# Sliding-window attention with an MLP on one core: weight loads on SP's queue, row-sum adds on ACT, sink copies first, and a new list for the first 21 steps

## The chip, the cores and the metric

The kernel runs on one core of one Trainium2 chip. The metric is the device time of one execution in microseconds (us). The kernel before was timed three times: 725.0, 724.87 and 722.57, median 724.87. A further execution, the one that was profiled, took 722.06.

## The reference

```python
def _attn_ref(q, k, v, n_sink, window):          # q, k, v: 4 x 8 x 768 x 64
    scores = scale * np.matmul(q, k.transpose(0, 1, 3, 2))
    keep = is_sink | in_window                   # first 4 keys, or the last 128 positions
    scores = np.where(keep, scores, -1000000000.0)
    scores = scores - np.max(scores, axis=-1, keepdims=True)
    a = np.exp(scores)
    a = a / (np.sum(a, axis=-1, keepdims=True) + 1e-09)
    return np.matmul(a, v)

def _moe_ref(x, w_in, w_out):                    # x: 3072 x 512, w_in: 512 x 2048
    h = x @ w_in
    g = np.maximum(h, 0.0) + np.log1p(np.exp(-np.abs(h)))
    return g @ w_out                             # w_out: 2048 x 512
```

The attention's output, heads side by side, is the `x` of the second part: softplus between two matrix products. The inputs are float32 except that the weights reach the kernel as 64-bit words.

## The kernel before, in words

**Tiling.** The 3072 tokens are 12 chunks of 256 rows, three for each of the four batches. A chunk has eight heads of attention (a head and chunk together are a *step*, 96 in all), and then, in slices that lie between the attention steps of the following chunk, the MLP: eight slices of 256 of the 2048 hidden columns. All weights stay in SBUF: 32 half blocks, `wi00` to `wi71` of w_in and `wo00` to `wo71` of w_out (the first digit is the slice, the second the half), each loaded as 512 KB of 64-bit words and turned into a high and a low part (`fp32r`), so that a product is three matmuls, high by high, low by high, high by low. Chunks 0 and 1 do their scores and values on plain float32 operands; from chunk 2 on these are split in two parts as well.

**What one step issues.** Each part has a letter that the list below uses, followed by a number (the step, or for `U F P R D E` the chunk's slice).

- `S` scores (L255 in chunks 0 and 1, L258 and L259 later): PE matmuls into `s`.
- `T` softmax: DVE masks the block above the diagonal (L271) and takes a masked row maximum (L277), ACT the exponential with its row sum `sm` (L278); each for two blocks of 128 rows.
- `N` normalise: 1e-9 is added to `sm` (L284, DVE), the reciprocal `rc` is taken (L285, DVE), the weights are multiplied by it (L290 on ACT, L292 on DVE or POOL).
- `W` weights_t: PE turns the weights (L326), a copy `th` of them is made (L59 on ACT, L61 on DVE), POOL makes the two triangles `pt` of it (L337, L340).
- `k` and `K`: the four sink keys' weights of four heads (`sa`, L297, DVE), turned by PE (`ts`, L308) and copied by ACT into the two halves of `sk` (L59). From chunk 2 on DVE subtracts each half from its source right behind its copy (L67). In chunks 0 and 1 POOL clears `sk` first (L311).
- `V` values: PE (L356, L362); `O` out: ACT writes the high part `xh` and DVE the low part `xl` of two heads of the MLP's input (L59, L67).
- `U` up: 24 matmuls `h` of a slice (L488); `F` softplus: three ACT passes (L495 to L497); `P` gate: maximum and sum on DVE (`mt`, L503) and its high part `gh`; `R`: the low part `gl` (DVE, L67); `D` and `E`: the slice's matmuls into `acc` (L525 to L527).
- `w`, `a`, `c`, `d`, `l`: the next half block of weights: its load (`_weight_dma`, L387 to L400), the cast of its words' top (`upper`), the combination with the rest (L432, DVE), the cast to the high part and the subtraction that gives the low part (L67).
- `G`, `L`, `j`, `J`, `p`, `q`: loads of values, keys and queries, of the sinks, and the splits of chunk 2's inputs.

**What sets the order.** `START` is a string of 362 such tokens that is written out by hand for the first 21 steps; behind it a loop over `STEADY` places the parts of each later step in a fixed order. On PE and SP (`ORDERED`) instructions stand exactly in the order of the tokens; on DVE, ACT and POOL a scheduler sets them at build time. All five engines then run their queues in order. Tables name the engine of the n-th operation of a kind (A is ACT, V is DVE, P is POOL; the last letter holds for all that follow): `NM` the multiply, `TH` the copy `th`, `GH` the cast `gh`, `WT` the cast of the top, `WH` the high part, `WL` the low part.

**Queues.** Keys, queries, values and results are issued by SP (`nc.sync.dma_start`, L200, L202, L207, L227), weights by ACT (`nc.scalar.dma_start`, L397), in ACT's own order of instructions, at 0.34 us for each issue. A transfer has one of eight completion semaphores in turn (`DMAHW0` to `DMAHW7` in the order of instructions below), and a new one waits until the transfer that last used its semaphore has landed.

Of the kernel before, what the change touches and what calls it, by code (L numbers as in the profile page):

```python
# [133 lines left out]
class _Attention:  # L134
# [145 lines left out]
    def normalise(self, h):  # L280
# [3 lines left out]
        nc.vector.tensor_scalar(sm[:], sm[:], 1e-9, None, ALU.add)  # L284
# [590 lines left out]
Ctx.START = """
S0 G4 T0 w w S1 j4 T1 J0 w L8 w w S3 S2 N0 N1 T2 W0 L10 w N2 S4 T3 N3 a w T4 k0 a c K0 a S5 c W1 w w
d S6 V0 O0 l d V1 w c l T5 N4 W2 T6 d w a S7 c O1 W3 l N5 G6 N6 a T7 c V2 N7 a d S8 k4 a O2 W4 w T8
c V3 S9 O3 w w K4 d l l V4 W5 N8 L12 w O4 c T9 S10 W6 d T10 N9 V5 l O5 a c G8 S11 W7 d l T11 L14 w
W8 G10 V6 N10 V7 O6 N11 a c O7 d l w k8 a U0 w c a S12 d a l d w T12 c w d l l K8 V8 c F0 N12 O8 P0
a c d R0 l d a c w W9 U1 a S13 c F1 T13 l a d c l d a P1 l N13 d c D0 l w R1 a c G12 w V9 w w d L16  # L880
O9 l W10 U2 a w d S14 F2 a c l T14 c d l P2 d l N14 W11 a L17 c V10 a w c E0 U3 p16 O10 d w w w l w
R2 F3 d D1 a S15 E1 a T15 w c a P3 c E2 d a d c d G14 l N15 V11 c l l L18 O11 k12 l d U4 l W12 a S16
p17 F4 K12 R3 T16 c a D2 a a l D3 V12 d c c N16 P4 L19 O12 p18 S17 W13 c R4 a U5 d F5 l a E3 d T17 c
V13 l N17 c G16 P5 W14 p19 L20 l J16 O13 U6 D4 S18 F6 E4 d l T18 L21 R5 P6 l W15 R6 p20 U7 d D5 F7 d
# [55 lines left out]
```

## Time and profile before

| | |
|---|---|
| three runs | 725.0, 724.87, 722.57 us (median 724.87) |
| the profiled execution | 722.06 us |
| its span, from the first to the last instruction | 720.4 us |
| busy: PE, DVE, ACT, POOL | 692.9 (96%), 549.0 (76%), 453.1 (63%), 399.8 (56%) us |
| mean clock granted to PE | 0.992 |
| first matmul of slice 0 of chunk 0 (`U0`) | 40.05 us |
| first matmul of slice 0 of chunk 1 (`U8`, the last but a few in `START`) | 110.97 us |

PE is the engine for matmuls and PEld its weight loads, which overlap the matmuls; DVE, ACT and POOL are the vector, scalar and general engines; ACTq and SPq are the places where ACT and SP issue DMAs. `128x512 fp32r<-128x512 f32 x5 | 5.9, 1186 | 0.5 <-ACT wo L59 0.5` reads: five instructions of that shape, 5.9 us busy, 1186 ns each in the mean, 0.5 us of idle time of the engine ahead of them, and what ended most of it. Line numbers are those of the kernel before.

### The profile page before, as it was taken

The page shows a single profiled execution, that of the slowest core. Times are in us where ns is not written, and L with a number is a line of the kernel's source. Part 1 is how long each engine was busy: PE and PEld are TensorE (multiplying, and loading weights), DVE is VectorE, ACT ScalarE, POOL GpSimd, SP SyncE. Part 2 cuts the span into 40 slices and gives each one's busy share as a digit, 9 for nine tenths or more (in the row PEclk, how much of TensorE's full clock was granted, in tenths as well). Part 3 has the DMA queues.
Part 4 walks back from the last instruction along what each step waited for, and adds up shares of the span by engine and source line. Part 5 has one row for each costly group of instructions (what it writes and reads, how often), then busy time and mean ns, then how long its engine had stood idle before and what let it go on. Part 6 is the DMA issues. An engine that isn't in the chain of part 4 may idle for free.

```text
span 720.4 us, 13834 instructions
## 1 busy us (share of the span) xinstructions
PE 692.9 (96%) x4465; PEld 618.6 (86%) x4465; DVE 549.0 (76%) x1596; ACT 453.1 (63%) x1122; POOL 399.8 (56%) x769
## 2 busy tenths in 40 slices
PE   4788899999999999999999999999999999999996
...
GB/s 299 333 244 262 168 45 47 130 48 46 102 66 50 108 68 49 113 59 51 100 52 67 79 78 56 95 65 57 94 53 71 97 50 79 60 13 1 30 1 34
DMA packets 41204, 63.36 MB, mean 88 GB/s; under 512 B 4644, under 2 KB 22692, under 8 KB 41124
## 3 DMA queue, kind: packets, MB, share of 16 engines
...
## 4 chain that ended last, share of the span: by engine, by line
PE 90%; DVE 3%; ACT 2%; DMA 2%; POOL 1%; issue 1%; SPq 0%; ACTq 0%; POOLq 0%
PE h L488 37%; PE acc L525 12%; PE acc L527 12%; PE acc L526 12%; PE x L362 6%; PE t L326 3%; PE s L258 3%; PE s L259 3%; PE x L356 2%; DMA wo71r<-w 1%; DMA q<-q 1%; ACT a L278 1%; DVE sm L284 1%; DMA words<-sizes 1%; DVE wt L432 0%
## 5 line engine op out<-in xcount | busy, mean ns | idle before, releaser
L488 PE MATMUL h<-xh,wi 128*128 128x256 f32 x1536 | 254.0, 288 | 0.0
L488 PEld LDWEIGHTS h<-xh,wi 128*128 128x128 f32 x1536 | 211.6, 191 | 1.2 <-issue 0.3
L488 PE MATMUL h<-xl,wi 128*128 128x256 f32 x768 | 154.6, 283 | 0.0
L525 PE MATMUL acc<-wo,gh 128*128 128x512 f32 x384 | 153.2, 399 | 0.0
L527 PE MATMUL acc<-wo,gl 128*128 128x512 f32 x384 | 151.2, 394 | 0.9 <-DVE gl L67 0.9
L526 PE MATMUL acc<-wo,gh 128*128 128x512 f32 x384 | 151.2, 394 | 0.0
L63 POOL TENSOR_SCALAR gh<-mt 128x512 fp32r<-128x512 f32 x91 | 57.3, 629 | 165.7 <-DVE mt L503 136.8
L495 ACT ACTIVATE mt<-h 128x512 f32<-128x512 f32 x96 | 57.5, 599 | 106.2 <-PE h L488 104.5
L292 POOL TENSOR_SCALAR a<-a,rc 128x128 f32<-128x128 f32 x180 | 72.4, 415 | 85.6 <-DVE rc L285 54.3
L488 PEld LDWEIGHTS h<-xl,wi 128*128 128x128 f32 x768 | 119.6, 192 | 0.0
L503 DVE SCALAR_TENSOR_TENSOR mt<-h,mt 128x512 f32<-128x512 f32 x96 | 65.8, 686 | 47.4 <-ACT mt L497 35.5
L278 ACT ACTIVATE a<-a,stats 128x136 f32<-128x136 f32 x192 | 76.0, 396 | 34.5 <-DVE stats L277 34.4
L527 PEld LDWEIGHTS acc<-wo,gl 128*128 128x128 f32 x384 | 72.4, 189 | 17.9 <-DVE gl L67 1.3
L525 PEld LDWEIGHTS acc<-wo,gh 128*128 128x128 f32 x384 | 72.4, 188 | 13.0 <-issue 0.5
L526 PEld LDWEIGHTS acc<-wo,gh 128*128 128x128 f32 x384 | 72.6, 189 | 9.3
L67 DVE TENSOR_TENSOR gl<-mt,gh 128x512 fp32r<-128x512 f32 x96 | 76.6, 798 | 4.9 <-POOL gh L63 4.6
L496 ACT ACTIVATE mt<-mt 128x512 f32<-128x512 f32 x96 | 60.8, 633 | 3.1
L497 ACT ACTIVATE mt<-mt 128x512 f32<-128x512 f32 x96 | 60.7, 633 | 3.1
L59 ACT CAST qkh<-qk 128x656 fp32r<-128x656 f32 x80 | 59.3, 741 | 1.5 <-DMA qk<-qk 1.4
L67 DVE TENSOR_TENSOR kl<-qk,qkh 128x400 fp32r<-128x400 f32 x80 | 52.3, 654 | 2.5
L271 DVE COPY_PREDICATED s<-diag,s 128x128 f32<-128x128 int32 x160 | 41.8, 290 | 15.4 <-PE s L259 12.5
L337 POOL TENSOR_SCALAR_AFFINE_SELECT pt<-th 128x256 fp32r<-128x256 f32 (+1 forms) x96 | 46.6, 486 | 8.0 <-DVE th L61 5.0
...
## 6 DMA issues: line engine op xcount, KB each, us to landing
...
out<-o SPq DMA_DIRECT2D x24, 256.0 KB, 2.6
q<-q SPq DMA_DIRECT2D x8, 256.0 KB, 5.9
...
k<-k SPq DMA_DIRECT2D x8, 200.0 KB, 4.4
wi00r<-w ACTq DMA_DIRECT2D x1, 511.8 KB, 4.8
wi01r<-w ACTq DMA_DIRECT2D x1, 511.8 KB
```

The source lines that it names most:

```text
L59: nc.scalar.copy(out, in_)
L67: (nc.vector if eng == "V" else nc.gpsimd).tensor_tensor(out, a, b, ALU.subtract)
L278: nc.scalar.activation(a, a, AF.Exp, bias=nm, scale=-1.0, accum_out=sm[:, j : j + 1])
L292: (nc.vector if eng == "V" else nc.gpsimd).tensor_scalar(a, a, rc[:, j : j + 1], 0.0, ALU.mult, ALU.add)
L488: nc.tensor.matmul(h[:, j], wt, x, start=k == 0, stop=k >= len(prods) - 2, skip_group_check=True)
L495: nc.scalar.activation(t[:], h[:], AF.Abs)
L496: nc.scalar.activation(t[:], t[:], AF.Exp, scale=-1.0)
L497: nc.scalar.activation(t[:], t[:], AF.Ln, bias=1.0)
L503: nc.vector.scalar_tensor_tensor(t[:], h[:], 0.0, t[:], ALU.max, ALU.add)
L525: nc.tensor.matmul(acc[:], gh[:, j, q], wh, start=f == 0, stop=False, skip_group_check=True)
L526: nc.tensor.matmul(acc[:], gh[:, j, q], wl, start=False, stop=False, skip_group_check=True)
L527: nc.tensor.matmul(acc[:], gl[:, j, q], wh, start=False, stop=f == 2 * FP - 1, skip_group_check=True)
```

## The change

Four edits are made together. The 1e-9 is added to the row sums by ACT (an Identity with a constant `tiny` as bias, which POOL writes once) where DVE did it, in all 96 steps. Both copies of `sk` are written ahead of the two subtractions. The 32 weight loads go to SP's queue, in the place of their `w` token among SP's other loads. `START` is a new order of the same 362 tokens, and the tables that name engines are new. `STEADY` is the same.

```diff
@@ normalise
-        nc.vector.tensor_scalar(sm[:], sm[:], 1e-9, None, ALU.add)
+        nc.scalar.activation(sm[:], sm[:], AF.Identity, bias=c.tiny[:, :1])
         nc.vector.reciprocal(rc, sm[:])
@@ sink
-        for j in range(CH):
-            r, q = slice(j * G * NS, (j + 1) * G * NS), slice(j * P, j * P + P)
+        places = [(slice(j * G * NS, (j + 1) * G * NS), slice(j * P, j * P + P)) for j in range(CH)]
+        for r, q in places:
             _copy(nc, "A", sk[r, q], t[r, :P])
-            if not self.exact:
+        if not self.exact:
+            for r, q in places:
                 _sub(nc, "V", sk[P // 2 + r.start : P // 2 + r.stop, q], t[r, :P], sk[r, q])
@@ _weight_dma
-        c.nc.scalar.dma_start(r[:, : 4 * WH - 1], src.bitcast(I16)[:, 1:])
+        c.nc.sync.dma_start(r[:, : 4 * WH - 1], src.bitcast(I16)[:, 1:])
@@ _kernel
+        c.tiny = c.const.tile([P, 1], F32, name="tiny")
+        nc.gpsimd.memset(c.tiny[:], 1e-9)
@@ tables
-Ctx.NM = "PPPAAPAPPVPPPPVVP"
-Ctx.TH = "AVAVAAAAVAAAAAVAVA"
-Ctx.GH = "VVVVVPPPP"
+Ctx.NM = "PPAPPPAAAAPPPPPPAPPPAP"
+Ctx.TH = "AAAAVVVAAVAAAAAAVAA"
+Ctx.GH = "PPVAAPAPAP"
-Ctx.WT = "PAAVVVVAVAAVAAAVAAAAAAAAAAAPAAAV"
-Ctx.WH = "VAPAAVAAAAVPPAAAAVVAVAAAAAVAVAAA"
-Ctx.WL = "PPPPPPPVPPVPPVPPVPVPPPPVVPVVPVPV"
+Ctx.WT = "VVAAPVPVAAPPAAPAAAAAAAAAAAAAAVAV"
+Ctx.WH = "AAPAAPAPPPAAVAVAAAAPAPAVPAAPAPAA"
+Ctx.WL = "VVPPVPPVVPPPPPVVPVVPVPVVVPPVVVVP"
@@ START, first line of ten
-S0 G4 T0 w w S1 j4 T1 J0 w L8 w w S3 S2 N0 N1 T2 W0 L10 w N2 S4 T3 N3 a w T4 k0 a c K0 a S5 c W1 w w
+S0 J0 w T0 N0 w w w w w L8 G6 S1 G4 T1 w j4 w S2 w L10 w w w T2 N1 L12 w w N2 L14 w W0 w w S3 T3 S4 T4 w a c a
```

Counted over `START` and by the tables, operations of each kind on each engine, before and after: multiplies by the reciprocal in 21 steps, two each: POOL 11 steps, ACT 3, DVE 3 before the table's last letter, and POOL 15, ACT 7; copies `th`: ACT 13, DVE 5, and ACT 14, DVE 5; casts `gh`: DVE 5, POOL 4, and POOL 5, ACT 4, DVE 1; tops: ACT 22, DVE 8, POOL 2, and ACT 21, DVE 6, POOL 5; high parts: ACT 21, DVE 8, POOL 3, and ACT 19, POOL 10, DVE 3; low parts: POOL 21, DVE 11, and DVE 17, POOL 15.

The first place is SP's queue where chunk 1's keys and queries (`k1_0` to `k1_6`, `q1_0` to `q1_6`) are loaded; `DMAHW` in brackets is the completion semaphore that the load waits for, `PE` that it waits for matmuls which read the buffer's former content. Before:

```order
L200 DMA k1_0_212<-k0 128x400 [waits DMAHW7_49]
L202 DMA q1_0_214<-q0 128x512 [waits DMAHW1_49]
L200 DMA k1_2_250<-k0 128x400 [waits DMAHW2_49,PE_49]
L202 DMA q1_2_252<-q0 128x512 [waits DMAHW3_49]
L227 DMA vr0_3_388<-v 128x2x128 [waits DMAHW4_49]
L200 DMA k1_4_481<-k0 128x400 [waits DMAHW7_49,DMAHW0_49,PE_49]
L202 DMA q1_4_483<-q0 128x512 [waits DMAHW1_49]
```

After, from `k1_4` on:

```order
L200 DMA k1_4_260<-k0 128x400 [waits DMAHW6_49,PE_49]
L202 DMA q1_4_262<-q0 128x512 [waits DMAHW7_49]
L398 DMA wo20r_264<-w 128x2047 [waits DMAHW0_49]
L398 DMA wo21r_266<-w 128x2047 [waits DMAHW1_49]
L200 DMA k1_6_272<-k0 128x400 [waits DMAHW2_49,PE_49]
L202 DMA q1_6_274<-q0 128x512 [waits DMAHW3_49]
L398 DMA wi40r_276<-w 128x2047 [waits DMAHW4_49]
L398 DMA wi41r_286<-w 128x2047 [waits DMAHW5_49]
L398 DMA wo30r_288<-w 128x2047 [waits DMAHW6_49]
```

Weight loads now stand between loads that wait for PE; of the 32, the twelve up to `wo21` are ahead of `k1_6` and the twenty from `wi40` on behind it.

The second place is ACT's queue around the sink weights of heads 0 to 3 (`sk0_0`), in the middle of chunk 0. Before, with weight loads among the casts:

```order
L397 DMA wi20r_275<-w 128x2047
L278 ACTIVATE a0_1_277,sm0_4_279<-a0_1_277,stats_63 128x136 x2
L59 CAST upper1_171<-wi01r_192 128x512
L59 COPY sk0_0_292<-ts0_0_290 32x128 x2
L59 CAST upper0_170<-wi10r_210 128x512
L397 DMA wi21r_311<-w 128x2047
L397 DMA wo10r_313<-w 128x2047
L59 CAST wi01_328<-wt0_0_1_301 128x512
L397 DMA wo11r_333<-w 128x2047
```

After, for the same place:

```order
L278 ACTIVATE a0_1_304,sm0_5_346<-a0_1_304,stats_63 128x136 x2
L59 CAST upper0_172<-wi10r_201 128x512
L59 CAST upper1_173<-wi11r_203 128x512
L59 COPY sk0_0_371<-ts0_0_369 32x128 x2
L284 ACTIVATE sm0_4_306<-sm0_4_306,tiny_66 128x2
L59 CAST wi01_380<-wt0_0_1_352 128x512
```

The loads have left the queue, and the add of head 4 stands behind the exponentials of head 5, two casts and the two copies of `sk`.

The third place is DVE's queue where slice 0 of chunk 0 is gated (`mt0_0`). Before:

```order
L432 SCALAR_TENSOR_TENSOR word_ps0_174<-wi30r_364,upper0_170 128x512
L61 CAST wi30_650<-word_ps0_174 128x512
L67 TENSOR_TENSOR wi30_650<-word_ps0_174,wi30_650 128x512
L432 SCALAR_TENSOR_TENSOR word_ps1_175<-wi31r_429,upper1_171 128x512
L284 TENSOR_SCALAR sm1_4_640<-sm1_4_640 128x2
L285 RECIPROCAL rc1_1_639<-sm1_4_640 128x2
L503 SCALAR_TENSOR_TENSOR mt0_0_666<-h0_0_596,mt0_0_666 128x512
L61 CAST gh0_0_677<-mt0_0_666 128x512
L432 SCALAR_TENSOR_TENSOR wt2_1_0_680<-wo20r_451,upper0_170 128x512
L67 TENSOR_TENSOR gl0_0_684<-mt0_0_666,gh0_0_677 128x512
```

After:

```order
L67 TENSOR_TENSOR wi30_638<-word_ps0_176,wi30_638 128x512
L433 SCALAR_TENSOR_TENSOR wt2_1_1_703<-wo21r_266,upper1_173 128x512
L504 SCALAR_TENSOR_TENSOR mt0_0_680<-h0_0_655,mt0_0_680 128x512
L61 CAST wo20_741<-wt2_1_0_684 128x512
L67 TENSOR_TENSOR wi31_653<-word_ps1_177,wi31_653 128x512
L433 SCALAR_TENSOR_TENSOR wt4_0_0_744<-wi40r_276,upper0_172 128x512
```

The cast `gh0_0`, the cast of `wi30` and the add of `sm1_4` have left DVE's queue; the reciprocal of head 4 of chunk 1 stands later in it. (`wt`, `word_ps0` and `word_ps1` are the combined words, `wi30r` is a half block as loaded, and the numbers behind the last underscore only tell tiles apart.)

More of the change, by code (lines that the diff above doesn't have):

```diff
@@ L396, in _weight_dma @@
     if c.w64:
-        c.nc.scalar.dma_start(r[:, : 4 * WH - 1], src.bitcast(I16)[:, 1:])
+        c.nc.sync.dma_start(r[:, : 4 * WH - 1], src.bitcast(I16)[:, 1:])
     else:
-        c.nc.scalar.dma_start(r[:, :WH], src)
+        c.nc.sync.dma_start(r[:, :WH], src)
     c.raw[s, k, half] = r
@@ L866 @@
 Ctx.GB, Ctx.EXACT = 3, 2
-Ctx.NM = "PPPAAPAPPVPPPPVVP"
-Ctx.TH = "AVAVAAAAVAAAAAVAVA"
-Ctx.GH = "VVVVVPPPP"
+Ctx.NM = "PPAPPPAAAAPPPPPPAPPPAP"
+Ctx.TH = "AAAAVVVAAVAAAAAAVAA"
+Ctx.GH = "PPVAAPAPAP"
 Ctx.WM = "sssssssppsppssssssssssssssssssss"
-Ctx.WT = "PAAVVVVAVAAVAAAVAAAAAAAAAAAPAAAV"
-Ctx.WH = "VAPAAVAAAAVPPAAAAVVAVAAAAAVAVAAA"
-Ctx.WL = "PPPPPPPVPPVPPVPPVPVPPPPVVPVVPVPV"
-Ctx.STEADY = ("kWUqYpKSFTRDVPONE", "SWTkpUKERDNFPqYVO")
-Ctx.START = """
-S0 G4 T0 w w S1 j4 T1 J0 w L8 w w S3 S2 N0 N1 T2 W0 L10 w N2 S4 T3 N3 a w T4 k0 a c K0 a S5 c W1 w w
@@ L877 @@
[L877 to L881, printed above, removed]
@@ L882 @@
-R2 F3 d D1 a S15 E1 a T15 w c a P3 c E2 d a d c d G14 l N15 V11 c l l L18 O11 k12 l d U4 l W12 a S16
-p17 F4 K12 R3 T16 c a D2 a a l D3 V12 d c c N16 P4 L19 O12 p18 S17 W13 c R4 a U5 d F5 l a E3 d T17 c
-V13 l N17 c G16 P5 W14 p19 L20 l J16 O13 U6 D4 S18 F6 E4 d l T18 L21 R5 P6 l W15 R6 p20 U7 d D5 F7 d
-N18 V14 S19 V15 L22 q16 O14 T19 P7 G18 O15 E5 S20 N19 k16 W16 T20 N20 R7 U8 K16 F8 P8 E6 p21 D6 V16
-O16
+Ctx.WT = "VVAAPVPVAAPPAAPAAAAAAAAAAAAAAVAV"
+Ctx.WH = "AAPAAPAPPPAAVAVAAAAPAPAVPAAPAPAA"
@@ new lines @@
+Ctx.WL = "VVPPVPPVVPPPPPVVPVVPVPVVVPPVVVVP"
+Ctx.STEADY = (
+    "kWUqYpKSFTRDVPONE",
+    "SWTkpUKERDNFPqYVO",
+)
+Ctx.START = """
+S0 J0 w T0 N0 w w w w w L8 G6 S1 G4 T1 w j4 w S2 w L10 w w w T2 N1 L12 w w N2 L14 w W0 w w S3 T3 S4 T4 w a c a
+N3 w w w S6 S5 d W2 T5 c k0 S7 l a a c c G8 K0 a N4 d W1 d d T6 l l w w w a N5 N6 L16 V0 O0 T7 w w L19 w w c
+L17 a V1 O1 c G10 G12 G16 W3 w w w l d N7 w l S8 T8 k4 a W4 N8 V2 S9 T9 V3 c O3 K4 S10 d l a c d d W5 l T10 V4
+O4 W6 l V5 O5 a W7 c N9 d a S11 T11 c a c V6 V7 l N10 c O7 d d l N11 S12 k8 a a d U0 F0 c K8 T12 a l c U1 P0
```

6 lines of the change are left out of this document (added).

## The prediction

> **What bounds the kernel now.** I read the page first. Its second part cuts the span into 40 slices of 18 us.
>
> ```profile
> span 720.4 us, 13834 instructions
> PE   4788899999999999999999999999999999999996
> ```
>
> A digit is the busy share in tenths, 9 for 90% or more: PE is full from the sixth slice on but not in the first five, which is where `START` rules. The view of windows puts sizes to that; its columns are the window, its length, the busy time of PE, PEld, DVE, ACT and POOL with the number of instructions, PE's granted clock, the share of DMA time and GB/s.
>
> ```profile
> 0.00:40.00 40.00, 25.23 (x116) 16.71 (x116) 29.83 (x127) 21.74 (x75) 29.30 (x65) 0.96 0.89 311
> 40.00:111.00 71.00, 64.50 (x385) 53.02 (x383) 66.08 (x157) 51.62 (x114) 41.84 (x56) 0.95 0.55 174
> 111.00:700.00 589.00, 588.98 (x3895) 536.85 (x3894) 449.65 (x1308) 375.38 (x926) 327.42 (x647) 1.00 0.22 64
> ```
>
> From 111 to 700 us PE is busy for 588.98 of 589.00 us at full clock: nothing that the other engines gain or lose there shows in the time, as long as PE's cover holds. The time is then set by when PE gets into that stretch, that is by the first 111 us. From 40 to 111 PE lacks 6.50 us, and the clock of 0.95 costs 0.05 x 71 = 3.5 us more, so 10.0 us is the most that can be won there. The engine that paces this stretch is DVE, busy for 66.08 of 71.00 us; ACT and POOL have room. I mark it with two instructions of DVE, the low parts `xl` of the last two heads of chunk 0 and of chunk 1, and with the first matmul of `U0` and of `U8`.
>
> ```profile
> 41.59 0.41 DVE L67 TENSOR_TENSOR xl<-x,xh 128x256 fp32r<-128x256 f32 x1
> 109.35 0.42 DVE L67 TENSOR_TENSOR xl<-x,xh 128x256 fp32r<-128x256 f32 x1 [0.52 <-ACT xh L59]
> 40.05 0.74 PE L488 MATMUL h<-xh,wi 128*128 128x256 f32 x4
> 110.97 0.72 PE L488 MATMUL h<-xh,wi 128*128 128x256 f32 x4
> 42.00:109.77 67.77, 61.27 (x360) 49.97 (x360) 63.68 (x150) 49.79 (x111) 39.12 (x50) 0.95 0.55 172
> ```
>
> Between the ends of the two `xl`, at 42.00 and 109.77 us, lie 67.77 us, of which DVE is busy for 63.68 and idle for 4.09. `U8` follows the second by 1.20 us. So the time is, to within PE's order of work, the length of DVE's list between the two marks.
>
> **The change part by part.** DVE's groups between the marks, which the change makes longer or shorter:
>
> ```profile
> L284 DVE TENSOR_SCALAR sm<-sm 128x2 f32<-128x2 f32 x8 | 1.5, 185 | 0.0
> L61 DVE CAST gh<-mt 128x512 fp32r<-128x512 f32 x5 | 3.0, 606 | 0.2
> L292 DVE TENSOR_SCALAR a<-a,rc 128x128 f32<-128x128 f32 x4 | 1.0, 283 | 0.1
> L61 DVE CAST wo<-wt 128x512 fp32r<-128x512 f32 x3 | 1.5, 492 | 0.0
> L61 DVE CAST wi<-word_ps 128x512 fp32r<-128x512 f32 x1 | 0.7, 691 | 0.0
> L61 DVE CAST upper<-wo71r 128x512 f16<-128x512 bf16 x1 | 0.5, 453 | 0.0
> L432 DVE SCALAR_TENSOR_TENSOR wt<-wo11r,upper 128x512 int32<-128x512 int32 x1 | 0.7, 676 | 0.0
> L67 DVE TENSOR_TENSOR wi<-word_ps,wi 128x512 fp32r<-128x512 f32 x3 | 2.0, 683 | 0.0
> L67 DVE TENSOR_TENSOR kl<-qk,qkh 128x400 fp32r<-128x400 f32 x5 | 3.6, 711 | 0.2
> L67 DVE TENSOR_TENSOR qkh<-qk,qkh 64x256 fp32r<-64x256 f32 x5 | 2.8, 552 | 0.2
> L67 DVE TENSOR_TENSOR wi<-wt,wi 128x512 fp32r<-128x512 f32 x4 | 2.8, 693 | 0.1
> L67 DVE TENSOR_TENSOR wo<-wt,wo 128x512 fp32r<-128x512 f32 x5 | 5.9, 1186 | 0.5 <-ACT wo L59 0.5
> L61 DVE COPY th<-t 128x256 f32<-128x256 f32 x1 | 0.4, 415 | 0.0
> ```
>
> I counted DVE's rows between the same two `xl` in both orders. What leaves the stretch: 7 adds x 0.185 = 1.3 us; 4 casts `gh` x 0.606 = 2.4; 4 multiplies x 0.283 = 1.1; one high part of `wi` at 0.691 and two of `wo` at 0.492, 1.7; one top, 0.5. Moved ahead of it or behind it rather than removed: three combinations x 0.676 = 2.0, one gate, priced like them, 0.7, two subtractions on `word_ps` x 0.683 = 1.4, and one head pair's split, 0.711 + 0.552 = 1.3. Together 12.4. What enters: two subtractions of `wi` x 0.693 and one of `wo` at 1.186, 2.6; a cast `th` and its low part, which I take at the copy's 0.415 each, 0.8; two reciprocals and one product `sa`, about 0.5 by the price of the adds. Together 3.9. The list is shorter by 8.5 us: 67.8 - 8.5 = 59.3 us, if DVE idles for 4.09 us as it does now.
>
> PE needs less than that: of its 61.27 us, the two passages at half clock take 3.4 (below), and the new list leaves two things behind `U8` that stood ahead of it, the second half block of slice 5 (`E5`) and the scores of step 20:
>
> ```profile
> 108.84 0.50 PE L525 MATMUL acc<-wo,gh 128*128 128x512 f32 x1
> 110.83 0.38 PE L326 MATMUL t<-ident,a 128*128 128x128 f32 x2
> ```
>
> From the first matmul of `E5` to the transpose behind step 20's scores are 1.99 us. PE's need is thus 61.3 - 3.4 - 2.0 = 55.9 us, so DVE stays the pacer, by 3.4 us. Those 2.0 us aren't won, only moved behind `U8`: an earlier `U8` by 8.5 us brings the end forward by 6.5.
>
> The start of the stretch I leave where it is. An add of that length stands on the chain of waits; behind it are the row of all adds (shortest, median and longest in ns) and those of ACT's own work:
>
> ```profile
> 31.15 0.92 DVE sm L284
> L284 DVE TENSOR_SCALAR sm<-sm x20: 155/164/991, 9.3 to 109.7; 128x2 f32<-128x2 f32 x20
> L278 ACT ACTIVATION_READ_ACCUMULATOR a<-a,stats 128x1 f32 x40 | 7.5, 187 | 0.0
> L290 ACT ACTIVATE a<-a,rc 128x128 f32<-128x128 f32 x6 | 2.1, 394 | 3.1 <-DVE rc L285 3.1
> L59 ACT COPY sk<-ts 32x128 f32<-32x128 f32 x8 | 2.0, 250 | 0.3 <-PE ts L308 0.3
> L59 ACT CAST wo<-wt 128x512 fp32r<-128x512 f32 x10 | 6.1, 612 | 2.2 <-DVE wt L432 2.1
> L59 ACT CAST upper<-wi10r 128x512 f16<-128x512 bf16 x1 | 0.8, 775 | 0.0
> ```
>
> That the adds leave DVE could bring the start forward: the one at 31.15 us held the chain for 0.92 us, where the median is 0.164. That the three combinations which leave the stretch go ahead of the first `xl` could put it back by 2.0 us. I let these two cancel and keep 2 us either way. An add on ACT lies between the 0.187 of the smallest row and the 0.394 of 128 columns; two columns are nearest to the former, 0.2.
>
> ACT in the stretch: 9 adds x 0.2, 3 casts `gh` x 0.612, a copy and two multiplies at about 0.39 come in, 4.8; four high parts x 0.612, two tops x 0.775 and a split (0.7) go, 4.7. Its 49.79 us stay, in 59.3 us rather than 67.8, 84%, and its 16 DMA issues there leave, which aren't in the busy time. ACT is no bound, but it is queued, and that is the unknown cost: the reciprocal, on DVE, must now wait for ACT's add. Where the add stands behind two tops and two copies of `sk`, it comes 2 x 0.775 + 2 x 0.250 = 2.1 us after the exponential. Nine reciprocals stand between the marks. At nothing (all stand late enough in DVE's list) to three full waits, 6.3 us; behind a waiting reciprocal DVE's masks, combinations and low parts stand, for which PE and POOL wait. I take one such wait, 2 us, since the new list puts other DVE work between most exponentials and their reciprocals.
>
> Sum: 8.5 - 2.0 - 2 = 4.5 us. The profiled execution, 722.06, becomes 717.6. It lies 2.8 below the median of 724.87; the mean of all four is 723.6, from which I predict 723.6 - 4.6 = **719.0 us**, rounded.
>
> At nothing I cost the sink copies' order (only from chunk 2 on, under PE's 588.98 of 589.00) and the adds of later steps (about 75 x 0.2 = 15 us of ACT, of whose 589.00 us 375.38 are busy). Without that cover two copies of 0.250 per sink would show.
>
> The subtractions that come to DVE are the price most open:
>
> ```profile
> L67 POOL TENSOR_TENSOR wo<-wt,wo 128x512 fp32r<-128x512 f32 x10 | 14.8, 1486 | 9.9 <-ACT wo L59 4.3 <-ACT mt L496 3.1 <-DVE wo L61 2.4
> ```
>
> A subtraction of `wo` takes 1.186 us on DVE and 1.486 on POOL, one of `wi` on DVE 0.693, with the same shape; so 0.5 us of waiting is in the first already. The Trainium skill, "SBUF — State Buffer", section "SBUF: two separate sides", says that DVE and GpSimd share a port pair as an exclusive lock, and that a DVE operation with two SBUF inputs waits for the whole of a GpSimd one that reads SBUF. By that rule three more subtractions would each be liable to such a wait, about 0.5 us each by the rows, 1.5 in all against the 0.5 that I have for `wo`, and the sum would be 3.5 rather than 4.5. The three `wi` rows at 0.683 show that it isn't the rule for each one.
>
> PE's half clock stands behind gaps:
>
> ```profile
> 46.45 0.66 PE L356 MATMUL x<-sk,vsf 128*64 128x256 f32 x2 [2.25 <-POOL sk L311]
> 63.27 1.34 PE L362 MATMUL x<-pt,vr 128*64 128x128 f32 x6 [1.85 <-POOL pt L340]
> ```
>
> After 2.25 us and after 1.85 us of waiting PE ran at half clock for 3.41 us each, 1.7 us lost per gap. The Trainium skill, "TensorE: Matmul & The Clock Gate", section "Part 1: The HAM clock gate", wants an idle window of about 3.4 us for that; the trace disagrees, and by the page's figure gaps of 2 us would cost only themselves.
>
> **The rivals.** *No change.* Each reciprocal is on DVE, and DVE runs in order; three full waits of 2.1 us cost 6.3, and the gain is 8.5 - 2.0 - 6.3 = 0.2 us: 723.4. For it speaks that the add's place in ACT's queue is set by a scheduler among 0.6 to 0.8 us casts; against it, ACT's 16% of free time.
>
> *Slower.* SP's queue is one row, and `k1_6` in it waits for the scores of heads 2 and 3 of chunk 1, whose inputs share its buffer; all weights from `wi40` on stand behind.
>
> ```profile
> 36.05 1.16 PE L255 MATMUL s<-k,q 128*128 128x264 f32 x4
> 37.24 0.33 SPq L200 DMA_DIRECT2D k<-k  x1
> wi40r<-w ACTq DMA_DIRECT2D x1, 511.8 KB, 6.1
> k<-k SPq DMA_DIRECT2D x8, 200.0 KB, 4.4
> q<-q SPq DMA_DIRECT2D x8, 256.0 KB, 5.9
> ```
>
> (The last three give a load's count, size and time from issue to landing.) Those scores ended at 37.2 us, and the load was issued then. Ahead of it and with it go 12 x 0.512 + 8 x 0.456 = 9.8 MB, 32 us at 311 GB/s, so that the queue runs dry at about 37; `wi40`, behind it, would land at 37.2 + 6.1 = 43.3 and is combined 15 rows of DVE behind `xl`, by 0.3 us a row at about 47. So 4 us of delay are free. To be slower than 728.5, the delay must take back the gain and 4.9 more: 4 + 4.6 + 4.9 = 13.5 us, scores not before 50.7 us. The price at 52 us is 723.6 - 4.6 + (14.8 - 4) = 729.8. Against it: the new list has these scores ahead of `U0`, so they can't be 14 us late unless the whole start is.
>
> **How the numbers follow.** Forecast 0.60, no change 0.29, slower 0.11. 0.5% (3.6 us) is about what a measurement of this kernel can tell from no change. Faster by more than that is below 721.2, the forecast and its neighbourhood: 0.60. Within it is the rival with the waits: 0.29. Slower is 0.11. The range: at the low end no wait at all and a start 2 us earlier, 723.6 - 6.5 - 2 = 715.1, less 1.6 for the scatter of the runs before (722.06 to 725.0, about half of it), 713.5; at the high end the rival without gain, 723.4, with 2 us of late start and a little of that scatter, 726.0. Left out are most of the slower case and the tips.
>
> **What would show it.** Right: `U8` at 40.05 + 1.95 + 59.3 + 1.2 + 2 = 104.5 us rather than 110.97; DVE's stretch between the marks about 61 us; adds at L284 on ACT at 0.2 us; PE full from then on, with an end 4.5 us earlier. Waits of DVE on "ACT sm" of 6 us and an unmoved `U8` show the first rival. Waits of DVE on "DMA", a wait of SP's queue on PE before `k1_6` beyond 45 us and `U8` later than 115 show the second. I am wrong, too, if PE, not DVE, is seen waiting for itself in the stretch, or if PE gets gaps behind 111 us.

## The result, and the profile after

The kernel after takes 707.40 us (median of four runs, 706.56 to 708.67), the kernel before 724.42 (four runs, 722.57 to 725.0): a ratio of 0.977, with a 95% interval of 0.975 to 0.980. The forecast was 719.0 with a range of 713.5 to 726.0. The direction was right and the size was not: 17.0 us instead of 4.6 to 5.4. The two profiled executions are 707.65 and 722.06, 14.4 us apart, since the one of before was the fastest of its four; their spans, 705.9 and 720.4, are 14.5 us apart, and these are compared from here on. Two executions lie far outside all others of their kernel (975.9 us of before, 2387.2 us in one of the runs below) and are in no figure of this text. In the kernel after, lines from 313 to 847 are one further down (L488 is L489, L432 is L433).

The page after, the slices of 18 us again:

```profile
span 705.9 us, 13834 instructions
PE   5899999999999999999999999999999999999996
```

PE is full from the third slice on instead of the sixth. The view of windows, with the columns as above:

```profile
0.00:40.00 40.00, 29.23 (x133) 19.73 (x134) 30.93 (x123) 28.34 (x98) 28.85 (x66) 0.91 0.86 302
40.00:111.00 71.00, 69.92 (x459) 60.39 (x458) 64.78 (x160) 60.04 (x145) 51.25 (x72) 1.00 0.55 184
111.00:690.00 579.00, 579.00 (x3836) 528.79 (x3836) 430.69 (x1206) 383.30 (x982) 320.07 (x634) 1.00 0.22 65
40.02:97.87 57.85, 56.77 (x380) 48.81 (x378) 53.28 (x129) 49.67 (x119) 40.68 (x53) 1.00 0.64 214
```

From 40 to 111 us PE lacks 1.08 us where it lacked 6.50, and its clock is 1.00 instead of 0.95. The last row is the stretch between the ends of the two `xl`, which are here, with the first matmuls of `U0`, of `U8` and of the block after `U8` (slice 1 of chunk 1, which I call `U9`):

```profile
39.60 0.42 DVE L67 TENSOR_TENSOR xl<-x,xh 128x256 fp32r<-128x256 f32 x1
97.46 0.41 DVE L67 TENSOR_TENSOR xl<-x,xh 128x256 fp32r<-128x256 f32 x1
38.13 0.83 PE L489 MATMUL h<-xh,wi 128*128 128x256 f32 x4
94.94 0.64 PE L489 MATMUL h<-xh,wi 128*128 128x256 f32 x4
103.73 0.72 PE L489 MATMUL h<-xh,wi 128*128 128x256 f32 x4
```

`U8` begins at 94.94 us, not at the 104.5 of the forecast, and 2.93 us *ahead* of the end of the `xl` that it was to follow by 1.20. PE's work ahead of `U9` is the same in both kernels (the same matmuls), so `U9` is the better mark: 117.51 before, 103.73 after, 13.78 us. From there to the first slice of the last chunk the kernel after wins 1.29 us more (544.78 instead of 546.07), and the end gives 0.6 back. Term by term:

| term of the sum | forecast | measured |
|---|---|---|
| end of chunk 0's last `xl`, 42.00 us | unmoved | 40.02, 2.0 earlier |
| DVE's stretch from there to chunk 1's last `xl`, 67.77 us | 61.3, 6.5 shorter | 57.85, 9.9 shorter |
| `U8` against that `xl`, 1.20 us behind | the same | 2.93 ahead, 4.1 gained |
| work left behind `U8` | -2.0 | -2.2 (the gain is 16.03 at `U8`, 13.78 at `U9`) |
| all behind `U9` | 0 | +1.3, and -0.6 at the end |
| sum | 4.5 | 14.5 |

Of the 13.78 us, 1.92 are won ahead of `U0` and 11.86 between `U0` and `U9`, which are these windows, before and after:

```profile
40.05:117.51 77.46, 70.95 (x427) 58.99 (x426) 69.39 (x171) 55.12 (x124) 44.29 (x62) 0.96 0.51 159
38.13:103.73 65.60, 64.52 (x425) 55.66 (x424) 59.52 (x148) 56.34 (x139) 48.22 (x67) 1.00 0.61 203
```

PE lacks 6.51 us of the first and 1.08 of the second, 5.4 us less, and it is busy for 6.4 us less. Two estimates fill those 6.4: the two passages at half clock cost 3.4 us, by the prediction, and the values of two heads that adjoin in the new list save up to 3.0, as an experiment below shows.

### The profile page after: what moved, and what is told of

Read it like the earlier page. It is cut to its first block, busy times and chain, and to the rows that moved or that the text cites. A ratio compares the mean times of both kernels' runs of the same rounds, so it can differ in the third digit from the quotient of the medians.

```text
span 705.9 us, 13834 instructions
## 1 busy us (share of the span) xinstructions
PE 687.3 (97%) x4465; PEld 616.3 (87%) x4465; DVE 528.5 (75%) x1489; ACT 474.1 (67%) x1228; POOL 400.8 (57%) x771
## 4 chain that ended last, share of the span: by engine, by line
PE 87%; DMA 4%; ACT 3%; DVE 3%; issue 1%; POOL 1%; SPq 1%; ACTq 0%; POOLq 0%
PE h L489 36%; PE acc L528 12%; PE acc L526 12%; PE acc L527 12%; PE x L363 5%; PE t L327 3%; PE s L258 3%; PE s L259 3%; PE x L357 1%; DMA wi50r<-w 1%; ACT a L278 1%; DMA qk<-qk 1%; DMA vr<-v 1%; DMA q<-q 1%; DVE wt L433 0%
## 5 line engine op out<-in xcount | busy, mean ns | idle before, releaser
L489 PE MATMUL h<-xh,wi 128*128 128x256 f32 x1536 | 253.9, 287 | 0.1
L489 PEld LDWEIGHTS h<-xh,wi 128*128 128x128 f32 x1536 | 211.2, 191 | 1.6 <-ACT xh L59 0.3
L489 PE MATMUL h<-xl,wi 128*128 128x256 f32 x768 | 154.6, 283 | 0.0
L496 ACT ACTIVATE mt<-h 128x512 f32<-128x512 f32 x96 | 57.5, 599 | 104.5 <-PE h L489 104.0
L489 PEld LDWEIGHTS h<-xl,wi 128*128 128x128 f32 x768 | 119.4, 191 | 0.1
L292 POOL TENSOR_SCALAR a<-a,rc 128x128 f32<-128x128 f32 x178 | 70.0, 407 | 68.0 <-DVE rc L285 64.4
L278 ACT ACTIVATE a<-a,stats 128x136 f32<-128x136 f32 x192 | 75.8, 396 | 20.2 <-DVE stats L277 20.1
L67 DVE TENSOR_TENSOR gl<-mt,gh 128x512 fp32r<-128x512 f32 x96 | 74.9, 780 | 4.8 <-POOL gh L63 4.4
L59 ACT CAST qkh<-qk 128x656 fp32r<-128x656 f32 x80 | 59.3, 742 | 0.4 <-DMA qk<-qk 0.2
L381 DVE TENSOR_TENSOR xt<-x,xt 64x256 f32<-64x256 f32 x80 | 33.2, 415 | 26.6 <-ACT xt L59 26.0
```

The costliest lines, as they stand in the source:

```text
L59: nc.scalar.copy(out, in_)
L67: (nc.vector if eng == "V" else nc.gpsimd).tensor_tensor(out, a, b, ALU.subtract)
L278: nc.scalar.activation(a, a, AF.Exp, bias=nm, scale=-1.0, accum_out=sm[:, j : j + 1])
L292: (nc.vector if eng == "V" else nc.gpsimd).tensor_scalar(a, a, rc[:, j : j + 1], 0.0, ALU.mult, ALU.add)
L489: nc.tensor.matmul(h[:, j], wt, x, start=k == 0, stop=k >= len(prods) - 2, skip_group_check=True)
L496: nc.scalar.activation(t[:], h[:], AF.Abs)
```

## The experiments

My theory, in the expectations as "List theory", was that the new order fills PE and that the edits to the code matter little; the rivals were that the loads' queue or the add on ACT makes the gain. The times in the table are medians, the ratios are to runs of the kernel before beside them (medians of 723.3 to 724.4), with their 95% intervals; `U0` and `U9` are read off each run's timeline of PE.

| kernel | `U0` | `U9` | between | us | ratio to before |
|---|---|---|---|---|---|
| before | 40.05 | 117.51 | 77.5 | 724.4 | 1 |
| after | 38.13 | 103.73 | 65.6 | 707.4 | 0.977 [0.975, 0.980] |
| list and tables only | 60.03 | 126.72 | 66.7 | 730.8 | 1.010 [1.008, 1.011] |
| three edits only | 50.63 | 126.99 | 76.4 | 730.3 | 1.010 [1.008, 1.011] |
| loads on SP only | 49.58 | 126.84 | 77.3 | 729.4 | 1.007 [1.005, 1.010] |
| add on ACT only | 45.65 | 121.91 | 76.3 | 730.1 | 1.009 [1.007, 1.012] |
| sink copies first only | 41.17 | 118.61 | 77.4 | 722.4 | 0.999 [0.998, 1.000] |
| after, loads back on ACT | 57.20 | 122.16 | 65.0 | 726.5 | 1.004 [1.003, 1.006] |
| after, add back on DVE | 38.90 | 106.88 | 68.0 | 710.4 | 0.983 [0.981, 0.985] |
| after, all old tables | 44.25 | 120.73 | 76.5 | 723.4 | 1.000 [0.999, 1.002] |
| after, old weight tables | 40.85 | 115.72 | 74.9 | 719.1 | 0.994 [0.992, 0.995] |
| after, old attention tables | 40.74 | 106.91 | 66.2 | 709.9 | 0.982 [0.980, 0.983] |

But for 1.3 us of the sink copies, no part is worth anything alone: the list with its tables, the loads by themselves and the add by itself each make the kernel some 6 to 7 us *slower*. Together the four edits make it 17 us faster.

**The list and its tables alone** (the old `normalise`, `sink` and `_weight_dma`, the new tables and `START`):

```diff
-Ctx.NM = "PPPAAPAPPVPPPPVVP"
+Ctx.NM = "PPAPPPAAAAPPPPPPAPPPAP"
...
-S0 G4 T0 w w S1 j4 T1 J0 w L8 w w S3 S2 N0 N1 T2 W0 L10 w N2 S4 T3 N3 a w T4 k0 a c K0 a S5 c W1 w w
+S0 J0 w T0 N0 w w w w w L8 G6 S1 G4 T1 w j4 w S2 w L10 w w w T2 N1 L12 w w N2 L14 w W0 w w S3 T3 S4 T4 w a c a
```

> The kernel before with the new list and tables alone (weight loads stay on ACT's queue, the add on DVE, the old order of the sink copies). If the gain of 17.0 us comes from the order of the work (List theory), 709 to 713 us. If it needs the loads off ACT's queue (Queue theory), at least 717 us, with ACT's issues waiting for semaphores in front of its casts. If it needs the add off DVE (Add theory), about 713 to 716 us, with 20 adds of 0.3 us back on DVE.

Measured: 730.8 us. My theory falls as it stands, and the queue theory holds. This run's rows of ACT's waits and of the windows:

```profile
ACT a L278 <- DMA vr<-v: 6.6, 1, 6.6
ACT wi L59 <- DMA wo20r<-w: 4.4, 1, 4.4
ACT xh L59 <- DMA wo40r<-w: 3.6, 1, 3.6
ACT a L278 <- DMA k<-k: 3.2, 1, 3.2
0.00:40.00 40.00, 15.88 (x51) 10.48 (x51) 17.26 (x82) 13.68 (x47) 14.58 (x43) 0.77 0.97 357
```

An exponential (L278) does not need a load of values or keys. It stands behind a weight load whose semaphore that transfer still holds, and the new list has its weight loads so early that ACT stands at them for 18 us. PE is busy for 15.88 of the first 40 us instead of 29.23. The loads themselves aren't held up: the DMA share is 0.97, more than the 0.86 of the kernel after. The transfers take their turn in both kernels; here ACT's casts and exponentials wait along with them.

**The three edits without the list** (the old tables and the old `START` in the kernel after):

```diff
-Ctx.START = """ S0 J0 w T0 N0 w w w w w L8 G6 ...
+Ctx.START = """ S0 G4 T0 w w S1 j4 T1 J0 w L8 w w ...
```

> The three edits to the code with the old list and the old tables. List theory: 721 to 724 us, of which 1.3 us are the gain that the traces show behind 104 us. Queue theory: 715 us or less. Add theory: 718 to 720 us, since the 20 adds of 0.330 us in the first 111 us leave DVE, which paced that stretch.

730.3 us, slower than any of the three theories had it. Two runs further down take the edits apart.

**The loads back on ACT, all else as after:**

```diff
-        c.nc.sync.dma_start(r[:, : 4 * WH - 1], src.bitcast(I16)[:, 1:])
+        c.nc.scalar.dma_start(r[:, : 4 * WH - 1], src.bitcast(I16)[:, 1:])
```

> The kernel after with the 32 weight loads back on ACT's queue. List theory: no more than the 32 issues of 0.34 us can cost, and of those only what ACT has on the path, so 707 to 710 us. Queue theory: 716 us or more.

726.5 us, as the queue theory had it. The table shows where: `U0` is 19 us late, while from `U0` to `U9` it takes 65.0 us, no longer than in the kernel after. So the two halves of the gain are apart: the list with its tables shortens the stretch by 11 to 12.5 us on either queue (66.7 and 65.0 us with the loads on ACT, 65.6 on SP), and the queue decides whether the list's early loads cost 19 us ahead of it. The 65.0 us aren't a clean measure of the list, though: with `U0` so late the other engines had time to run ahead.

**The add back on DVE, all else as after:**

```diff
-        nc.scalar.activation(sm[:], sm[:], AF.Identity, bias=c.tiny[:, :1])
+        nc.vector.tensor_scalar(sm[:], sm[:], 1e-9, None, ALU.add)
```

> The kernel after with the 1e-9 added on DVE again. List theory: PE has work from 40 us on and waits for 1.1 us only, so the adds come out of DVE's slack: 707 to 709 us. Add theory: 6.6 us for 20 adds of 0.330 us, so 711 to 714 us.

710.4 us, 3.0 slower by the medians, between the two theories: a part of 6.6 us of adds was in DVE's slack.

**The sink copies first, alone:**

```diff
         for r, q in places:
             _copy(nc, "A", sk[r, q], t[r, :P])
-            if not self.exact:
+        if not self.exact:
+            for r, q in places:
                 _sub(nc, "V", sk[P // 2 + r.start : P // 2 + r.stop, q], t[r, :P], sk[r, q])
```

> The kernel before with both sink copies ahead of the subtractions and nothing else changed. The traces of before and after differ by 13.78 us at the second slice of chunk 1's MLP and by 15.06 at the last chunk's, so 1.3 us come behind it, in steps of 0.15 to 0.3 us once or twice in each batch. If the sink copies' order gives them: 722.2 us here, with the value matmul of the step behind the sinks 0.2 to 0.3 us shorter. If the add gives them (rival): no change, 723.5 us.

722.4 us; the whole time doesn't tell it from before (the interval reaches 1.000). The trace does, since it starts 1.1 us later and ends 0.3 earlier: from `U9` to the last chunk's first slice it takes 544.70 us, against 546.07 before. The runs with the new order of copies have 544.68 to 544.78 there (after, the three edits, the loads back on ACT, the add back on DVE), those with the old one 545.52 (the list alone) and 546.07 (the loads alone). The steps lie at the values of one head, here in before, then after:

```profile
232.74 0.28 PE L356 MATMUL x<-sk,vs 128*128 128x256 f32 x1
233.04 0.73 PE L362 MATMUL x<-pt,vv 128*128 128x256 f32 x3
```

```profile
218.89 0.28 PE L357 MATMUL x<-sk,vs 128*128 128x256 f32 x1
219.01 0.63 PE L363 MATMUL x<-pt,vv 128*128 128x256 f32 x3
```

The second matmul starts 0.30 us behind the first instead of 0.12: PE waits for `pt`, which POOL ends at 232.98 us, and the view of PE shows it as busy. With 588.98 of 589.00 us busy there were still 1.3 us to win.

**The loads on SP alone** and **the add on ACT alone**, each put into the kernel before:

```diff
-        c.nc.scalar.dma_start(r[:, : 4 * WH - 1], src.bitcast(I16)[:, 1:])
+        c.nc.sync.dma_start(r[:, : 4 * WH - 1], src.bitcast(I16)[:, 1:])
```

> The kernel before with its weight loads on SP's queue and nothing else changed. The three edits together with the old list gave 730.3 us. If SP's queue is what costs there (a load of keys that waits for PE holds the weights behind it, the mechanism of my slower rival), this run alone gives 728 to 732 us, with SP waiting for PE's scores about 12 us and the first slice's matmul near 50 us. If the add on ACT costs it, this run gives 723 us.

```diff
-        nc.vector.tensor_scalar(sm[:], sm[:], 1e-9, None, ALU.add)
+        nc.scalar.activation(sm[:], sm[:], AF.Identity, bias=c.tiny[:, :1])
```

> The kernel before with the 1e-9 added on ACT and nothing else changed. The same edit is worth 3.0 us in the new list. If it takes as much off DVE here, 720.5 us; if DVE's reciprocals wait behind ACT's loads and casts (my no-change rival), 723 to 726 us.

729.4 and 730.1 us. The first is my slower rival: SP's waits for PE, a wait of DVE for a load behind them, and SP's queue around one of its waits.

```profile
SPq L200 <- PE t L326: 19.8, 2, 14.0
33.58 0.46 DVE L61 CAST upper<-wo01r 128x512 f16<-128x512 bf16 x1 [3.53 <-DMA wo01r<-w]
39.48 0.33 SPq L397 DMA_DIRECT2D wi40r<-w  x1
40.79 0.38 SPq L227 DMA_DIRECT2D vr<-v  x1
46.77 0.33 SPq L200 DMA_DIRECT2D k<-k  x1
47.15 0.43 SPq L202 DMA_DIRECT2D q<-q  x1
47.62 0.43 SPq L397 DMA_DIRECT2D wi41r<-w  x1
```

`k1_6` is issued at 46.8 us, and `wi41` can only be behind it. An earlier such wait, of 14.0 us, holds all that stands behind it until 25.5 us; DVE then stands 3.5 us at the cast of `wo01`, PE waits 5.6 us for DVE's row maxima behind it, and `U0` is at 49.58. (Here the profile puts these waits down to PE's transposes, not to the scores that I expected; in the run with all three edits it puts 12.2 us down to the scores.) The second is my no-change rival, and worse. DVE's waits for the add, here and in the kernel after up to 104 us (the total, how many, the longest):

```profile
DVE rc L285 <- ACT sm L284: 14.8, 12, 2.8
```

```profile
DVE rc L285 <- ACT sm L284: 3.8, 5, 1.1
```

In the old list reciprocals stand right behind their exponentials and wait for 14.8 us in all; the new one has moved them back. The add alone costs 3.0 us behind `U9`, too (549.02 against 546.07), which the new order of sink copies takes away: with all three edits it is 544.78.

**The tables.** The first of three runs has all six old tables in the kernel after, the second the first two of them, the third the other four:

```diff
-Ctx.NM = "PPAPPPAAAAPPPPPPAPPPAP"
-Ctx.TH = "AAAAVVVAAVAAAAAAVAA"
+Ctx.NM = "PPPAAPAPPVPPPPVVP"
+Ctx.TH = "AVAVAAAAVAAAAAVAVA"
...
-Ctx.GH = "PPVAAPAPAP"
-Ctx.WT = "VVAAPVPVAAPPAAPAAAAAAAAAAAAAAVAV"
-Ctx.WH = "AAPAAPAPPPAAVAVAAAAPAPAVPAAPAPAA"
-Ctx.WL = "VVPPVPPVVPPPPPVVPVVPVPVVVPPVVVVP"
+Ctx.GH = "VVVVVPPPP"
+Ctx.WT = "PAAVVVVAVAAVAAAVAAAAAAAAAAAPAAAV"
+Ctx.WH = "VAPAAVAAAAVPPAAAAVVAVAAAAAVAVAAA"
+Ctx.WL = "PPPPPPPVPPVPPVPPVPVPPPPVVPVVPVPV"
```

> The kernel after with the engine tables of before (more multiplies, casts and tops on DVE, as many as before). If DVE's list paces the start, as I forecast, the 7 us or so that the tables take off it come back, 714 us. If the list's order and early loads make the gain and PE paces, DVE's slack takes them, 708 to 710 us.

> The kernel after with the old tables for the multiplies and for the copies of the turned weights, the other four as after. With all six old tables the gain of 16 us was gone. If it is the sum of DVE's work, these two put back about 1.1 us (four multiplies of 0.283): 708.5 us. If it is where a single operation falls in its engine's queue, no sum tells it: half of the 16 us, 711 to 719 us.

> The kernel after with the old tables for the gate's casts and for the weights' tops, high and low parts. By the sum of DVE's work these put back 2.4 + 1.7 + 0.5 - 2.6 = 2.0 us: 709.5 us. By the place in the queues: half of the 16 us or more, 711 to 723 us, with waits of ACT, DVE and POOL for each other's parts of a half block.

723.4, 709.9 and 719.1 us. The first loses all of the gain, 16.0 us, where DVE is busy for 9.5 us more ahead of `U9` (98.13 against 88.60, rows below). Two more runs took one of these lines each, the last (`WL`, low parts) and that of `GH` (gate casts):

> The kernel after with the old table for the low parts alone: six fewer of them on DVE in the start, six more on POOL. By the sum of DVE's work (2 x 1.186 + 4 x 0.693 = 5 us less on DVE) it is as fast or faster, 703 to 707.4 us. If it counts when a half block is ready (POOL takes 1.34 to 1.49 us for a low part and does them one after the other), slower: 710 to 716 us, with PE waiting for low parts from POOL.

> The kernel after with the old table for the gate's casts alone: five of the first nine on DVE instead of one. By the sum of DVE's work: 4 x 0.606 = 2.4 us at most, 709.8 us. If DVE has slack there: 707.4 to 708.5 us. If the place in the queues decides: more than 711 us.

714.9 us (ratio 0.989, 0.987 to 0.991) and 709.95 (0.984, 0.980 to 0.987, six runs from 709.1 to 717.0). The gate casts cost 2.5 us by the medians, which is the number of the sum; but in the trace of that run PE waits 2.7 us for a load of values and 2.1 for an `xl`, where it waits 0.4 and nothing in the kernel after, so the sum isn't shown to be the reason. The low parts don't fit the sum. In the traces six of them go from DVE to POOL (DVE has 19 after, 13 before and here; the 17 and 11 given with the change are letters of the table, and some low parts go to DVE whatever their letter), 3 to 5 us of work, and the kernel is 7.5 us slower. DVE isn't even relieved. The windows up to `U9` in the kernel after, in this run and with all old tables:

```profile
0.00:103.73 103.73, 91.88 (x541) 73.56 (x542) 88.60 (x265) 82.80 (x230) 75.32 (x130) 0.97 0.70 239
0.00:111.42 111.42, 92.08 (x542) 73.78 (x542) 90.23 (x259) 83.31 (x230) 81.90 (x137) 0.97 0.65 223
0.00:120.73 120.73, 95.90 (x541) 75.66 (x542) 98.13 (x276) 81.15 (x220) 71.53 (x126) 0.93 0.62 206
```

DVE has six instructions less and is busy for 1.6 us more. The rows of this run's chain of waits, then of PE's timeline:

```profile
98.33 0.54 ACT wo L59
98.89 1.82 DVE wo L67
100.71 0.40 DVE s L271 x2
...
103.62 0.42 DVE xl L67
```

```profile
103.07 0.74 PE L489 MATMUL h<-xh,wi 128*128 128x256 f32 x4 [2.65 <-ACT xh L59]
```

A low part on DVE stands waiting for ACT's high part, everything behind it in DVE's queue waits along, and `U8`'s last heads come 2.65 us too late. The low part itself takes 1.82 us, where 0.68 is usual: a low part on POOL runs from 98.87 to 100.16 us, and DVE's ends 0.55 us behind that. Nine subtractions and combinations of 128x512 on DVE took more than 1.2 us in this run ahead of `U9`, four in the kernel after, and all of them show the same (more on it below). What counts is which operation stands in front of the one that PE needs, and which one it meets on the other engine, not the length of the list.

**The values of a pair apart.** In the kernel after, `V8` and `V9`, `V10` and `V11`, `V12` and `V13`, `V14` and `V15` adjoin on PE; here a block stands between them.

```diff
-... a V8 l d l l V9 O8 d c W10 ...
+... a V8 l d l l W10 V9 O8 d c ...
```

> The kernel after with another matmul block between the values of the two heads of each pair in chunk 1. The traces show two heads' values in 2.2 us where they adjoin and in 1.5 us each where they don't. If PE paces the kernel after from 40 us on, that is 4 x 0.8 = 3.2 us, 710.5 us. If DVE still paces it (my forecast's picture), 707.4 to 708 us.

708.8 us (ratio to before 0.979, 0.977 to 0.981), 1.4 slower by the medians, but the intervals of the two kernels overlap; in the traces `U9` comes 2.2 us later. Two adjoining heads in the kernel after, then a head that stands alone in the kernel before:

```profile
52.86 0.65 PE L357 MATMUL x<-sk,vsf 128*64 128x256 f32 x2
...
53.57 0.43 PE L357 MATMUL x<-sk,vsf 128*64 128x256 f32 x1
...
55.01 0.44 PE L327 MATMUL t<-ident,a 128*128 128x128 f32 x2
```

```profile
54.95 0.65 PE L356 MATMUL x<-sk,vsf 128*64 128x256 f32 x2
55.44 1.03 PE L362 MATMUL x<-pt,vr 128*64 128x128 f32 x6
56.40 0.44 PE L326 MATMUL t<-ident,a 128*128 128x128 f32 x2
```

The second head starts at 53.57 us, in the middle of the first. A pair takes 2.15 us, one head 1.45, so adjoining saves 0.75 us a pair and 3.0 in the chunk. A part of that shows in the time: PE and the engines that feed it are about even in this stretch. The Trainium skill, "TensorEngine Tiling (Array Packing)", section "Tiling Modes", lists 128x64 as two tiles that can work in parallel, and its section "Overview" gives a small dimension of up to 64 at most twice the speed; here it is 2.90 to 2.15, 1.35 times.

**How much `U8`'s lead is worth.** `U8` may start ahead of `xl` since only its last six matmuls use the last two heads' rows (the expectation says eight), and only the last two of those the low parts `xl`. Here they come first:

```diff
-        prods = [(e, cc, j) for cc in range(4) for e in ("hh", "lh", "hl") for j in range(2)]
+        ccs = (3, 0, 1, 2) if self.chunk == 1 and s == 0 else range(4)
+        prods = [(e, cc, j) for cc in ccs for e in ("hh", "lh", "hl") for j in range(2)]
```

> The kernel after, in which slice 0 of chunk 1 multiplies the last two heads' rows first instead of last (one matmul block's inner order). After's trace has this block begin at 94.94 us, 2.9 us ahead of the end of the low parts that its last eight matmuls need. If that lead is part of the gain, the block must now wait until 97.3 us: 2 to 2.5 us slower, 709.5 to 710 us. If the block follows the low parts anyway, as my sum had it, no change, 707.4 us.

712.6 us, 5.2 slower (four runs from 711.4 to 715.7). PE's waits from 40 us on (lines behind the edit are one further down in this run):

```profile
PE x L363 <- DMA vr<-v: 3.8, 1, 3.8
PE h L490 <- ACT xh L59: 2.2, 1, 2.2
```

The second is the lead; the first has nothing to do with it. A load of chunk 1's values, issued at 61 us behind a load that waits for DVE, lands when PE wants it, a little before or after. To take it out, the load was put ahead of the waiting one (about 4 us earlier), with and without the last heads first, and then ahead of two such loads (at 45.6 us), again both ways:

```diff
-... N5 N6 L16 V0 O0 T7 w w L19 w w c L17 a V1 O1 c G10 G12 G16 ...
+... N5 N6 L16 V0 O0 T7 w w L19 w w c G10 L17 a V1 O1 c G12 G16 ...
...
-... N5 N6 L16 V0 O0 T7 w w L19 w w c L17 a V1 O1 c G10 G12 G16 ...
+... N5 N6 G10 L16 V0 O0 T7 w w L19 w w c L17 a V1 O1 c G12 G16 ...
```

> The kernel after with one load of chunk 1's values put ahead of the load of chunk 2's queries, keys that stands in SP's queue waiting for a split. In after's trace PE waits 0.44 us for this load, in the run with the last heads first 3.8 us. If SP's queue is the cause of both, this version is 0.5 us faster than the kernel after, 706.9 us, and no run of it waits for values; if the load is late for want of bandwidth, no change.

> The same, and slice 0 of chunk 1 multiplies the last two heads first. That run was 5.2 us slower than the kernel after, where I had expected 2 to 2.5; its trace shows 2.2 us of waiting for the last heads and 3.8 for the values. If the values' load made the excess: 709.5 to 710.5 us. If the lost lead costs it all, through the half clock behind the gap: 712 us.

> The kernel after with the load of chunk 1's second pair of values ahead of both loads of chunk 2 that follow it, issued at about 46 us instead of 61. Moved by 4 us only, it still landed 9.3 us after its issue, and PE waited 1.1 us for it. If its late issue makes PE's waits for values (0.44 us after, up to 3.8 in other runs), they are gone here: 706 to 707 us, and all runs within 1.5 us. If it is something else, waits for values and their scatter stay.

> The same, and slice 0 of chunk 1 multiplies the last two heads first. Without waits for values the cost of the lost lead stands alone: 2.2 us of waiting and up to 1.7 for the half clock behind the gap, so 2.2 to 3.9 us over the run beside it, 709 to 710.5 us. No difference, if the block follows the low parts anyway, as my sum had it.

Four microseconds earlier did not do: 706.7 us with a wait of 1.1 us left, and 707.6 to 714.2 with the last heads first (median 710.0), with a wait of 3.1 us. In the first of these the load took 9.2 us from issue to landing instead of 6.1, so that it landed only 0.7 us earlier. At 45.6 us the wait is gone: 706.2 us (705.1 to 707.3) and 709.5 (707.5 to 711.4). The block in both, and the windows around it:

```profile
92.92 0.63 PE L489 MATMUL h<-xh,wi 128*128 128x256 f32 x4
90.00:105.00 15.00, 14.96 (x99) 13.28 (x97) 13.32 (x37) 13.12 (x36) 10.94 (x19) 1.00 0.13 36
```

```profile
95.61 0.76 PE L490 MATMUL h<-xh,wi 128*128 128x256 f32 x4 [2.19 <-ACT xh L59]
90.00:105.00 15.00, 12.81 (x71) 11.06 (x68) 10.17 (x32) 10.25 (x30) 9.67 (x17) 0.89 0.12 36
```

The lead is worth 3.3 us by the medians and 4.0 by `U9` (105.66 against 101.67): 2.19 us of waiting and 0.11 x 15 = 1.65 of clock behind it. The clock's part isn't there each time: in the run with the load 4 us earlier the block has the same gap of 2.19 us, and the clock granted from 97 to 107 us is 1.00. The version without the last heads first is the fastest here, 706.2 us at a ratio to before of 0.977 (0.974 to 0.979); against the kernel after's 0.977 (0.975 to 0.980) its 1.2 us are no shown gain, only its missing wait is.

## Why the prediction was wrong, point by point

- **What bounds the kernel.** That only the start can move was right: 13.78 of 14.5 us are won ahead of `U9`. "10.0 us is the most that can be won there" held for PE's waits and clock from 40 to 111 us, but it took PE's work as given (the pairs of values, up to 3.0 us) and left out the 14.8 us that PE lacked in the first 40, of which 10.8 are left.
- **DVE's list.** The step "the time is the length of DVE's list between the two marks" is the one that failed. The stretch came out at 57.85 us instead of 61.3: DVE's busy time is 53.28 us, where the sum gave 55.2, and its idle time 4.57 where I had 4.09 + 2. The term most mis-sized is a low part of `wo`, taken at 1.186 us, which is 0.711 in the kernel after:

```profile
L67 DVE TENSOR_TENSOR wo<-wt,wo 128x512 fp32r<-128x512 f32 x6 | 4.1, 711 | 0.0
L67 DVE TENSOR_TENSOR wi<-wt,wi 128x512 fp32r<-128x512 f32 x6 | 4.0, 696 | 3.1 <-POOL wi L63 3.1
```

  Six of them are 2.9 us cheaper. The five in the prediction's row took 0.69, 1.77, 0.90, 0.89 and 1.68 us, so 1.186 wasn't the price of a low part of `wo`: it holds two long waits. The prediction took it that 0.5 us of waiting are in it, and this is so, but it priced the new one the same. The waits are for POOL, here in before and, for a combination, in the kernel after:

```profile
60.60 1.27 POOL L67 TENSOR_TENSOR wi<-wt,wi 128x512 fp32r<-128x512 f32 x1
60.64 1.77 DVE L67 TENSOR_TENSOR wo<-wt,wo 128x512 fp32r<-128x512 f32 x1
```

```profile
66.25 1.72 POOL L67 TENSOR_TENSOR wo<-wt,wo 128x512 fp32r<-128x512 f32 x1
66.76 1.76 DVE L433 SCALAR_TENSOR_TENSOR wt<-wi60r,upper 128x512 int32<-128x512 int32 x1
```

  DVE's instruction begins while POOL's runs and ends 0.55 us behind POOL's end. So do all subtractions and combinations of 128x512 on DVE over 1.2 us ahead of `U9`, four in either kernel. The Trainium skill, "SBUF — State Buffer", section "SBUF: two separate sides", says that whichever of the two starts first has the shared ports for its whole instruction, and that this concerns operations of DVE with two inputs in SBUF; these rows agree. The three `wi` rows at 0.683, by which the prediction doubted the rule, read `word_ps`, which lies in PSUM. POOL was busy for 40.68 of those 57.85 us, but only one of the six `wo` low parts in the kernel after began while it ran, and that one took 0.88 us. Which operations meet is not told by their count: the sum of 3.5 us, with a wait for each, was further off.
- **`U8` behind `xl`.** This 1.20 us was read off one place and kept as a rule; it is 4.1 us of the error. The rows quoted in the prediction spoke against it: `U0` at 40.05 us is 1.95 ahead of the end of *its* `xl`. In the kernel before, `U8` stood late for another reason, the blocks ahead of it on PE. The lead by itself is worth 3.3 us (the pair of runs above).
- **The start.** "I let these two cancel and keep 2 us either way": it was 2.0 us earlier, the edge of that.
- **PE behind DVE.** I had DVE pace by 3.4 us (59.3 against a need of 55.9). PE is busy for 56.77 of 57.85 us and waits for about 1: it had become the pacer, or even with DVE. The run with the add back on DVE shows about half of its price, that with the values apart 1.4 us by the medians and 2.2 by `U9` of 3.0, which says the same.
- **What was left behind `U8`.** 2.0 forecast, 2.2 measured: right.
- **Edits costed at nothing.** The copies' order gave 1.3 us, and the add would have cost 3.0 behind `U9` without it. The cover, PE's 588.98 of 589.00, isn't what it seemed, since PE counts as busy while a matmul of a block waits.
- **The rivals.** Both mechanisms exist, and both appear in full with the old list: 14.8 us of waiting for the add, 19.8 of SP for PE. The new list is what makes them small, with 3.8 us for the former; in the kernel after SP waits for PE's scores too (11.1 us), and `wi40` is issued at 37.1 us, when I had the queue run dry. My argument that PE's scores are early enough held.
- **The way of adding.** The sum took each edit's price by itself. But for the sink copies no part alone is better than nothing, and the low parts' table shows a loss where the sum has a gain. An order written for one placement of operations is not a sum of prices. I can't work out from these runs how much of the 11.9 us between `U0` and `U9` each of list and tables has, only that the list with the old tables keeps 1.0 of them; the new tables under the old list were not run.
